# Strassen's algorithm for two of four products in a retention-and-gated-product kernel: one level of it, three stages that share memory, weights by quarters, clamps on ScalarE

## The chip, the cores and the metric

One core of one Trainium2 chip. The metric is the device time of the kernel in microseconds (us). Engines: PE (TensorE, products), DVE (VectorE), ACT (ScalarE), POOL (GpSimd), SP (SyncE, which issues the loads and stores). "Conversion" is what DVE does to the weights: they arrive as 64-bit floats and are turned into 32-bit ones by integer operations, in 40 blocks of 128 x 512.

## The reference

```python
scores = q @ k.T / sqrt(64)              # batch 8, heads 8, sequence 576, head width 64
x = (scores * decay_mask) @ v            # -> 4608 tokens x 512
a, b = x @ w1, x @ w2                    # 512 x 1024 each, float64 in memory
out = ((a * b) @ w3) @ w_out             # 1024 x 1024, 1024 x 512
```

The kernel multiplies w3 by w_out once and uses the product. Attention goes in 4 batch pairs of 5 chunks, 20 turns `g` in all.

## The kernel before: the parts that matter

```python
ld bufs={"k": 2, "q": 1, "v": 3}                # three v buffers

def convert_block():                             # 7 operations on DVE
    e = shift(hi); e = max(e - 896, 0); e = min(e, 255) * 2**23   # two clamps
    e |= sign(hi); m = mantissa(hi); m += lo * 2**-32; w = m * e

def up(i, n, f):                                 # 8 fp32 products of 384 columns
    for w in (w1_sb, w2_sb):
        for c in range(4): matmul(t, w[:, c, f*128:...], xT[:, c, n*384:...])
    scalar.copy(a, ps[0]); vector.tensor_mul(ab[:, f], ps[1], a)

for g in range(20):                              # one turn
    load(g + 2, "kv"); front(g + 1); load(g + 2, "q")
    convert_up_to(...); work(half of the waiting units)
    pv(g); state(g + 1); score(g + 1); work(the other half)
```

`front` multiplies q and v by the decay on POOL and transposes k and q on PE; `pv` is the value product; `work` runs `up` units and `down` groups (the last product) from a list. In the figures below `up` is the w1/w2 product, `po` the last product, `ps` w3 x w_out, `tp` a transpose, `xps` the value product, `sc` the scores, `st` the state.

## Time and profile before

| | before |
|---|---|
| median of 3 runs | 1036.15 us |
| span of the profiled run | 1032.4 us |
| PE busy | 966.2 us |
| end of w3 x w_out (end of the weights' work) | 290.4 us |
| sum of PE's holes before that | 62.5 us |
| sum of PE's holes after it | 0.0 us |

The last three rows come from PE's own instructions: the end of the last `ps`, and the times in which no PE instruction was open (the 3.7 us after PE's last instruction are not counted).

### The profile page before, as it was taken

What the parts mean: (1) busy time and instruction counts of PE and PEld (TensorE: products, weight loads), DVE (VectorE), ACT (ScalarE), POOL (GpSimd) and SP (SyncE); (2) the same over time, 40 slices, a digit from 0 to 9 for tenths busy, and PEclk for the clock granted to TensorE, in tenths of its full rate; (3) what the DMA queues carried; (4) which work ended last, traced back from release to release, by engine and by line L of the source; (5) the groups of instructions that cost most, each with busy time, mean ns of one, the idle gap of its engine ahead of it and who ended that gap; (6) DMA issues with size and microseconds to landing.
All of it is one profiled execution on the core that took longest, in us unless ns stands there. A gap on an engine that the chain in (4) does not pass through costs nothing.

```text
span 1032.4 us, 11355 instructions
## 1 busy us (share of the span) xinstructions
PE 966.2 (94%) x4933; PEld 570.8 (55%) x4933; DVE 269.3 (26%) x475; ACT 144.1 (14%) x285; POOL 78.4 (8%) x47
## 2 busy tenths in 40 slices
PE   4869998498899999999999999999999999999998
PEld 3855565245445565656656555646646545455553
DVE  4898456767800010101110100101101001000010
ACT  2320111011201111111111111202111110010100
POOL 3233010010010100110101101010100000000000
PEclk8888999698999999999999999999999999999999
DMA  7966312252300303212003103113000000000000
GB/s 175 239 171 172 83 50 93 81 143 83 104 29 31 72 1 82 52 31 62 21 11 82 32 11 82 43 40 73 1 21 11 1 31 0 21 11 7 24 0 31
DMA packets 124002, 59.51 MB, mean 58 GB/s; under 512 B 114216, under 2 KB 114216, under 8 KB 123952
## 3 DMA queue, kind: packets, MB, share of 16 engines
q1 hardware_dynamic: 122624, 58.73, 21.2%
q8 instruction: 39, 0.64, 0.3%
q10 hardware_dynamic: 1328, 0.06, 0.1%
q14 instruction: 11, 0.09, 0.0%
HBM read 49.34 MB, written 9.44 MB: 57 GB/s over the span
## 4 chain that ended last, share of the span: by engine, by line
PE 82%; DVE 12%; DMA 3%; issue 1%; SPq 1%; ACT 0%; ACTq 0%; POOL 0%; DVEq 0%; POOLq 0%
PE up L300 44%; PE po L311 24%; PE ps L287 4%; PE xps L196 3%; PE sc L148 3%; DVE e L255 2%; PE tp L133 2%; DMA raw<-in_moe_w_dram 2%; DVE m L260 2%; DVE e L250 2%; PE st L169 1%; DVE m L258 1%; PE xps L189 1%; DVE e L252 1%; DVE e L253 1%; DVE pm L151 1%
## 5 line engine op out<-in xcount | busy, mean ns | idle before, releaser
L300 PE MATMUL up<-xT,w_sb 128*128 128x384 f32 x1536 | 504.6, 489 | 5.4 <-DVE ab L305 5.4
L300 PEld LDWEIGHTS up<-xT,w_sb 128*128 128x128 f32 x1536 | 291.5, 191 | 208.2 <-DVE ab L305 6.6
L311 PE MATMUL po<-w3o,ab 128*128 128x512 f32 x576 | 249.8, 593 | 0.0
L305 DVE TENSOR_TENSOR ab<-up,a 128x384 f32<-128x384 f32 x96 | 53.2, 557 | 576.5 <-PE up L300 576.2
L311 PEld LDWEIGHTS po<-w3o,ab 128*128 128x128 f32 x576 | 109.0, 190 | 134.0 <-issue 130.8
L304 ACT COPY a<-up 128x384 f32<-128x384 f32 x96 | 45.9, 478 | 407.2 <-PE up L300 371.4
L122 POOL TENSOR_TENSOR ld_q<-ld_q,gq 128x1024 f32<-128x1024 f32 (+1 forms) x20 | 38.7, 1935 | 645.3 <-DMA ld_q<-in_q_dram 638.6
L151 DVE TENSOR_TENSOR pm<-sc,mask 128x512 f32<-128x512 f32 (+1 forms) x80 | 45.4, 629 | 134.8 <-PE sc L148 134.8
L287 PE MATMUL ps<-wo,w3T 128*128 128x512 f32 x128 | 60.3, 627 | 1.3 <-ACT w3T L280 1.3
L314 ACT COPY ot<-po 128x512 f32<-128x512 f32 x36 | 21.1, 585 | 250.7 <-PE po L311 230.2
L287 PEld LDWEIGHTS ps<-wo,w3T 128*128 128x128 f32 x128 | 25.3, 203 | 31.2 <-issue 28.3
L133 PE MATMUL tp<-ident,ld_q 128*128 128x128 f32 (+1 forms) x160 | 22.1, 287 | 20.1 <-POOL ld_q L122 20.1
L122 POOL TENSOR_TENSOR ld_v<-ld_v,gk 128x1024 f32<-128x1024 f32 (+1 forms) x20 | 39.5, 1975 | 2.3 <-DMA ld_v<-in_v_dram 2.3
L148 PE MATMUL sc<-qT,kT 64*128 64x128 f32 (+1 forms) x640 | 39.1, 273 | 0.0
L196 PE MATMUL xps<-pm,ld_v 128*64 128x128 f32 (+1 forms) x640 | 37.8, 273 | 0.0
L148 PEld LDWEIGHTS sc<-qT,kT 64*128 64x128 f32 (+1 forms) x640 | 35.4, 183 | 1.5 <-issue 0.5
L196 PEld LDWEIGHTS xps<-pm,ld_v 128*64 128x64 f32 (+1 forms) x640 | 33.4, 143 | 5.0 <-issue 5.0
L278 PE MATMUL tp<-ident,w 128*128 128x128 f32 x64 | 10.7, 303 | 25.2 <-DVE w L262 25.1
L255 DVE SCALAR_TENSOR_TENSOR e<-raw,e 128x512 int32<-128x512 int32 x40 | 32.6, 814 | 1.4
L133 PEld LDWEIGHTS tp<-ident,ld_q 128*128 128x128 f32 (+1 forms) x160 | 18.6, 153 | 21.4 <-POOL ld_q L122 21.4
L200 ACT COPY xT<-xps 128x512 f32<-128x512 f32 (+1 forms) x40 | 19.8, 546 | 73.0 <-PE xps L196 73.0
L260 DVE SCALAR_TENSOR_TENSOR m<-raw,m 128x512 f32<-128x512 uint32 x40 | 27.7, 693 | 1.4
(32 smaller groups left out, 296.8 us busy)
## 6 DMA issues: line engine op xcount, KB each, us to landing
raw<-in_moe_w_dram SPq DMA_DIRECT2D x24, 512.0 KB, 3.6
out_dram<-ot SPq DMA_DIRECT2D x36, 256.0 KB, 2.0
ld_k<-in_k_dram SPq DMA_DIRECT2D x16, 512.0 KB, 4.8
ld_v<-in_v_dram SPq DMA_DIRECT2D x16, 512.0 KB, 5.9
ld_q<-in_q_dram SPq DMA_DIRECT2D x16, 512.0 KB, 4.4
raw<-in_moe_w_dram SPq DMA_DIRECT2D x16, 256.0 KB, 4.9
raw<-in_moe_w_out_dram SPq DMA_DIRECT2D x8, 512.0 KB, 3.2
ld_k<-in_k_dram SPq DMA_DIRECT2D x4, 256.0 KB, 4.9
```

Of the source, the lines that this page charges most:

```text
L122: nc.gpsimd.tensor_tensor(out=t[:sz], in0=t[:sz], in1=gam[:sz, c].rearrange("p b h -> p (b h)").unsqueeze(2).to_broadcast([sz, 2 * H, D]), ...
L133: nc.tensor.transpose(tp[:, p, :sz], src[:sz, h:h + 2, :].rearrange("p a d -> p (a d)"), ident[:sz, :sz])
L148: nc.tensor.matmul(sc[j][:sz, p, :sz], kT[hs, b, p, :sz], qT[hs, b, p, :sz], start=True, stop=True)
L151: nc.vector.tensor_mul(pm[:sz, b, j, :, :sz], sc[j][:sz, :, :sz], mask[:sz, :sz].unsqueeze(1).to_broadcast([sz, NP, sz]))
L196: nc.tensor.matmul(banks[r][heads[half], b, n, :sz], vs[:sz, b * H + 2 * p + j, :], pm[:sz, b, j, p, :sz], start=(c == 0 and m == 0), stop ...
L255: vec.scalar_tensor_tensor(e, in0=hi, scalar=-(1 << 31), in1=e, op0=ALU.bitwise_and, op1=ALU.bitwise_or)
L260: vec.scalar_tensor_tensor(m.bitcast(F32), in0=lo.bitcast(U32), scalar=2.0 ** -32, in1=m, op0=ALU.mult, op1=ALU.add)
L287: nc.tensor.matmul(ps, live["w3T", ft][:, g, :], wo[:, g, :], start=(g == 0), stop=(g == KF - 1))
L300: nc.tensor.matmul(t, w[:, c, f * P:(f + 1) * P], xT[:, c, n * TB:(n + 1) * TB], start=(c == 0), stop=(c == KD - 1))
L304: nc.scalar.copy(a, ps[0])
L305: nc.vector.tensor_mul(live["ab", i, n][:, f, :], ps[1], a)
L311: nc.tensor.matmul(po, ab[:, f, t * P:(t + 1) * P], w3o[:, f, :], start=(f == 0), stop=(f == KF - 1))
```

## The change

Intent: PE bounds most of the run, so give it fewer columns. Strassen's form makes 7 block products out of 8; the sums go to POOL (weights and tokens) and DVE (results). In the code, S names the sums of weight quarters and T those of token quarters; a *unit* is one call of `up`. To find memory for the sums, the kernel runs in three stages whose tiles lie over each other: (1) first pair's attention and all of w1, w2; (2) the rest of the first pair's units, w_out and w3; (3) everything else. Weights are converted by quarters of columns so that units can start early, with two blocks in flight, and two of seven conversion steps go to ACT. The core of the diff, cut:

```diff
-            t = ld.tile(..., bufs={"k": 2, "q": 1, "v": 3}[nm])
+            t = pools["ld"].tile(...)                       # 2 of each
...
+    def strassen_weights(fp):                               # POOL, 512 elements each
+        tt("S1", "A21", "A22", ALU.add);  tt("S2", "S1", "A11", ALU.subtract)
+        tt("S3", "A11", "A21", ALU.subtract);  tt("S4", "A12", "S2", ALU.subtract)
...
-        vec.tensor_scalar(out=e, in0=e, scalar1=-896.0, scalar2=0.0, op0=ALU.add, op1=ALU.max)
-        vec.tensor_scalar(out=e, in0=e, scalar1=255.0, scalar2=2.0 ** 23, op0=ALU.min, op1=ALU.mult)
+        nc.scalar.activation(e, e, relu, bias=lim[:, 0:1], scale=-1.0)
+        nc.scalar.activation(e, e, relu, bias=lim[:, 1:2], scale=-2.0 ** 23)
...
+    def up(i, n, fp, conv=0):                               # a quarter: 28 products of 192
+        p1 = product(None, "A11", "B11");  nc.scalar.copy(p1s, p1)
+        u2 = plus("u2", product(None, "S2", "T2"), p1s)     # plus: DVE, then conv steps
+        u3 = plus("u3", product(None, "S3", "T3"), u2)
+        p5 = product(None, "S1", "T1")
+        plus("c22", p5, u3, out=c[:, 2])
+        plus("c21", product(None, "A22", "-T4"), u3, out=c[:, 1])
+        product(p1, "A12", "B21")                           # first result quarter, DVE
+        product(p5, "S4", "B22");  plus("c12", p5, u2, out=c[:, 0])
+        nc.gpsimd.tensor_tensor(out=ab[:, f + 1:f + 4, :], ...)   # other three, POOL
...
+    for g in range(NC):                                     # stage 1
+            load(g + 2, "kvq")
+        front(g + 1); pv(g); state(g + 1); score(g + 1); convert(10); up(0, 0, g - 1, conv=1); convert(6)
...
     for g in range(NC, G):                                  # stage 3: as before
             load(g + 2, "kv"); front(g + 1); load(g + 2, "q"); work(...); pv(g)
```

A wait that no line of the diff names follows from the first cut: with two v buffers, the load of v for turn g+2 overwrites the v of turn g, so SP holds it until `pv(g)` is done, and SP works in order.

More of the change, by code (lines that the diff above doesn't have):

```diff
@@ L59, with open_attention @@
     NB = 3
-    TB = 2 * S // NB
-    NT = TB // P
+    TB = S // NB
+    NT = 2 * TB // P
     KD = DM // P
     KF = DF // P
+    QC = CV // 2
+    NQ = DF // QC
     heads = [slice(j * D, (j + 1) * D) for j in range(2)]
     const = ctx.enter_context(tc.tile_pool(name="const", bufs=1))
-    raw = ctx.enter_context(tc.tile_pool(name="raw", bufs=2))
-    wst = ctx.enter_context(tc.tile_pool(name="wst", bufs=1))
-    ld = ctx.enter_context(tc.tile_pool(name="ld", bufs=2))
-    fr = ctx.enter_context(tc.tile_pool(name="fr", bufs=2))
-    xp = ctx.enter_context(tc.tile_pool(name="xp", bufs=2))
-    ffn = ctx.enter_context(tc.tile_pool(name="ffn", bufs=2))
+    wp = ctx.enter_context(tc.tile_pool(name="wp", bufs=1))
+    ffn = ctx.enter_context(tc.tile_pool(name="ffn", bufs=2))
+    xps = [ctx.enter_context(tc.tile_pool(name="xp0", bufs=1))]
+    weights_part, att_part, w3_part = ExitStack(), ExitStack(), ExitStack()
+    raw = weights_part.enter_context(tc.tile_pool(name="raw", bufs=2, side="right"))
+    ab3 = weights_part.enter_context(tc.tile_pool(name="ab3", bufs=1, side="right"))
+    pools = {}
+    def open_attention(part):
+        for nm in ("ld", "fr"):
+            pools[nm] = part.enter_context(
+                tc.tile_pool(name=nm, bufs=2, side="right", reuse_waits="tile"))
+    open_attention(att_part)
     acc = ctx.enter_context(tc.tile_pool(name="acc", bufs=7, space=PSUM))
@@ L83 @@
                             base=0, pattern=[[1, P]], channel_multiplier=-1)
+    lim = const.tile([P, 2], F32, tag="lim", name="lim")
+    nc.vector.memset(lim[:, 0:1], 1151.0)
+    nc.vector.memset(lim[:, 1:2], 255.0 * 2.0 ** 23)
     gk = const.tile([P, NC, 2, H], F32, tag="gk", name="gk")
     gq = const.tile([P, NC, 2, H], F32, tag="gq", name="gq")
-    dq = const.tile([H, S], F32, tag="dq", name="dq")
+    dq = ffn.tile([P, 3, 2, TB], F32, tag="c", name="dq").rearrange("p a b s -> p (a b s)")[:H, :S]
     nc.scalar.dma_start(dq, decay_q)
@@ L97, with A, tt @@
             nc.vector.tensor_copy(gq[:sizes[c], c, b, :], gps[:sizes[c], c, :])
-    w1_sb = const.tile([P, KD, DF], F32, tag="w1", name="w1_sb")
-    w2_sb = const.tile([P, KD, DF], F32, tag="w2", name="w2_sb")
-    w3o = const.tile([P, KF, DM], F32, tag="w3o", name="w3o")
-    wo = wst.tile([P, KF, DM], F32, tag="wo", name="wo")
+    halves = range(DF // CV)
+    wA = [wp.tile([P, 2, KD, CV], F32, tag=f"wA{h}", name="wA") for h in halves]
+    wS = [wp.tile([P, 3, 2, 2, 2, P], F32, tag=f"wS{h}", name="wS") for h in halves]
+    def A(fp, nm):
+        h, m = divmod(fp, 2)
+        if nm in ("S1", "S2", "S4"):
+            return wS[h][:, ("S1", "S2", "S4").index(nm), m]
+        r, f = {"A11": (0, 0), "A12": (1, 0), "A21": (0, 1), "S3": (0, 1), "A22": (1, 1)}[nm]
+        return wA[h][:, :, 2 * r:2 * r + 2, m * QC + f * P:m * QC + f * P + P]
+    def strassen_weights(fp):
+        def tt(out, in0, in1, op):
+            nc.gpsimd.tensor_tensor(out=A(fp, out), in0=A(fp, in0), in1=A(fp, in1), op=op)
+        tt("S1", "A21", "A22", ALU.add)
+        tt("S2", "S1", "A11", ALU.subtract)
+        tt("S3", "A11", "A21", ALU.subtract)
+        tt("S4", "A12", "S2", ALU.subtract)
     live = {}
@@ L110, in load @@
         for nm in names:
-            t = ld.tile([P, 2 * H, D], F32, tag="ld_" + nm, name="ld_" + nm,
-                        bufs={"k": 2, "q": 1, "v": 3}[nm])
+            t = pools["ld"].tile([P, 2 * H, D], F32, tag="ld_" + nm, name="ld_" + nm)
             nc.sync.dma_start(
@@ L125, in front @@
                 op=ALU.mult)
-        kT = fr.tile([P, 2, NP, P], F32, tag="kT", name="kT", bufs=1)
-        qT = fr.tile([P, 2, NP, P], F32, tag="qT", name="qT")
+        kT = pools["fr"].tile([P, 2, NP, P], F32, tag="kT", name="kT", bufs=1)
+        qT = pools["fr"].tile([P, 2, NP, P], F32, tag="qT", name="qT")
         for src, dst in ((kn, kT), (qn, qT)):
@@ L142, in score @@
         kT, qT = live["kT", g], live["qT", g]
-        pm = fr.tile([P, 2, 2, NP, P], F32, tag="pm", name="pm", bufs=1)
+        pm = pools["fr"].tile([P, 2, 2, NP, P], F32, tag="pm", name="pm", bufs=1)
         for b in range(2):
@@ L171, in state @@
                                      skip_group_check=True)
-        sb = fr.tile([P, 2, NP, D], F32, tag="sb", name="sb")
+        sb = pools["fr"].tile([P, 2, NP, D], F32, tag="sb", name="sb")
         nc.scalar.copy(sb, st)
@@ L178, in pv @@
         sz = sizes[c]
+        live["x", g] = True
         qT, vs, pm = live["qT", g], live["v", g], live["pm", g]
         if c == 0:
-            live["xT", i] = xp.tile([P, NP, 2, S], F32, tag="xT", name="xT")
+            live["xT", i] = xps[i > 0 and i % 2 == 0].tile([P, NP, 2, S], F32, tag="xT", name="xT")
         banks = [acc.tile([P, 2, 2, P], F32, tag="acc", name="xps") for r in range(2)]
@@ L205 @@
     blocks = []
-    for f0 in range(0, DF, CV):
-        for w_sb, w in ((w1_sb, moe_w1), (w2_sb, moe_w2)):
-            for c in range(KD):
-                blocks.append((("w12", f0, w is moe_w2, c), w, c, f0,
-                               lambda w_sb=w_sb, c=c, f0=f0: w_sb[:, c, f0:f0 + CV]))
-    for g in range(KF):
-        blocks.append((("wo", g), moe_w_out, g, 0, lambda g=g: wo[:, g, :]))
-    for ft in range(KF):
-        for g0 in range(0, DF, CV):
-            blocks.append((("w3", ft, g0), moe_w3, ft, g0,
-                           lambda ft=ft, g0=g0: w3_tile(ft)[:, g0:g0 + CV]))
-    at = {key: n for n, (key, *_) in enumerate(blocks)}
-    loaded, converted, turned = [0], [0], [0]
-    def w3_tile(ft):
-        if ("w3", ft) not in live:
-            live["w3", ft] = wst.tile([P, DF], F32, tag="w3", name="w3")
-        return live["w3", ft]
+    for fp in range(NQ):
+        for j, w in enumerate((moe_w1, moe_w2)):
+            for r in range(2):
+                blocks.append((("w12", fp, j, r), w))
+    blocks += [(("wo", g), moe_w_out) for g in range(KF)]
+    blocks += [(("w3", ft, g0), moe_w3) for ft in range(KF) for g0 in range(0, DF, CV)]
+    at = {key: n for n, (key, _) in enumerate(blocks)}
+    loaded, begun, converted, turned = [0], [0], [0], [0]
     def load_block():
@@ L228, in load_block @@
             return
-        key, w, r, c0, _ = blocks[n]
-        t = raw.tile([P, CV, 2], I32, tag="raw", name="raw")
-        if key[0] == "w12" and r >= NP // 2:
+        key, w = blocks[n]
+        t = raw.tile([P, CV, 2], I32, tag="raw", name="raw", bufs=4)
+        if key[0] == "w12":
+            _, fp, _, r = key
+            src = w[2 * r * P:2 * (r + 1) * P, fp * QC:(fp + 1) * QC, :]
             for half in range(2):
-                o = r * P + (1 - half) * D
-                nc.sync.dma_start(t[heads[half]], w[o:o + D, c0:c0 + CV, :])
+                for_rows = src.rearrange("(c a d) n t -> a d c n t", a=2, d=D)[half ^ r]
+                nc.sync.dma_start(t[heads[half]].rearrange("p (c n) t -> p c n t", c=2), for_rows)
         else:
+            r, c0 = (key[1], 0) if key[0] == "wo" else key[1:]
             nc.sync.dma_start(t, w[r * P:(r + 1) * P, c0:c0 + CV, :])
@@ L238, in load_block, with converted_to, begin_block @@
         loaded[0] += 1
-    def convert_block():
-        n = converted[0]
+    def converted_to(n):
+        key, _ = blocks[n]
+        if key[0] == "w12":
+            _, fp, j, r = key
+            return wA[fp // 2][:, j, 2 * r:2 * r + 2, fp % 2 * QC:fp % 2 * QC + QC]
+        if key[0] == "wo":
+            return live["wo"][:, key[1], :]
+        _, ft, g0 = key
+        if ("w3", ft) not in live:
+            live["w3", ft] = pools["wst"].tile([P, DF], F32, tag="w3", name="w3")
+        return live["w3", ft][:, g0:g0 + CV]
+    def begin_block():
+        n = begun[0]
         t = live["raw", n]
         lo, hi = t[:, :, 0], t[:, :, 1]
-        dst = blocks[n][4]()
-        e = raw.tile([P, CV], I32, tag="exp", name="e", bufs=1)
-        m = raw.tile([P, CV], I32, tag="man", name="m", bufs=1)
+        e = raw.tile([P, CV], I32, tag="exp", name="e")
+        m = raw.tile([P, CV], I32, tag="man", name="m")
         vec = nc.vector
@@ L251, in convert_block @@
                           op0=ALU.logical_shift_left, op1=ALU.logical_shift_right)
-        vec.tensor_scalar(out=e, in0=e, scalar1=-896.0, scalar2=0.0, op0=ALU.add, op1=ALU.max)
-        vec.tensor_scalar(out=e, in0=e, scalar1=255.0, scalar2=2.0 ** 23,
-                          op0=ALU.min, op1=ALU.mult)
+        relu = mybir.ActivationFunctionType.Relu
+        nc.scalar.activation(e, e, relu, bias=lim[:, 0:1], scale=-1.0)
+        nc.scalar.activation(e, e, relu, bias=lim[:, 1:2], scale=-2.0 ** 23)
@@ new lines, in begin_block, with end_block @@
+        yield
+        vec.tensor_scalar(out=m, in0=hi, scalar1=0x000FFFFF, scalar2=0x00100000,
+                          op0=ALU.bitwise_and, op1=ALU.bitwise_or)
+        yield
+        vec.scalar_tensor_tensor(m.bitcast(F32), in0=lo.bitcast(U32), scalar=2.0 ** -32, in1=m,
+                                 op0=ALU.mult, op1=ALU.add)
+        live["em", n] = e, m
+        begun[0] += 1
+        yield
+    def end_block():
+        n = converted[0]
+        hi = live["raw", n][:, :, 1]
+        e, m = live["em", n]
+        vec = nc.vector
@@ L255, in convert_block @@
         vec.scalar_tensor_tensor(e, in0=hi, scalar=-(1 << 31), in1=e,
                                  op0=ALU.bitwise_and, op1=ALU.bitwise_or)
-        vec.tensor_scalar(out=m, in0=hi, scalar1=0x000FFFFF, scalar2=0x00100000,
-                          op0=ALU.bitwise_and, op1=ALU.bitwise_or)
-        vec.scalar_tensor_tensor(m.bitcast(F32), in0=lo.bitcast(U32), scalar=2.0 ** -32, in1=m,
-                                 op0=ALU.mult, op1=ALU.add)
-        vec.scalar_tensor_tensor(dst, in0=m.bitcast(F32), scalar=2.0 ** -20,
-                                 in1=e.bitcast(F32), op0=ALU.mult, op1=ALU.mult)
@@ L264, in convert_block @@
-        converted[0] += 1
-        load_block()
+        yield
+        key = blocks[n][0]
+        while not (key[0] == "w12" or "wo" in live and (key[0] == "wo" or key[1] < turned[0] + 2)):
+            yield "wait"
+        out, m, e = converted_to(n), m.bitcast(F32), e.bitcast(F32)
+        if key[0] == "w12":
+            m, e = (x.rearrange("p (c n) -> p c n", c=2) for x in (m, e))
+        vec.scalar_tensor_tensor(out, in0=m, scalar=2.0 ** -20, in1=e, op0=ALU.mult, op1=ALU.mult)
+        converted[0] += 1
@@ new lines, in end_block, with conversion, convert @@
+        if n > 0:
+            load_block()
+        if key[0] == "w12" and key[2:] == (1, 1):
+            strassen_weights(key[1])
+        yield
+    def conversion():
+        yield from begin_block()
+        while converted[0] < len(blocks):
+            if begun[0] < len(blocks):
+                yield from begin_block()
+            yield from end_block()
+    converting = conversion()
+    def convert(n):
+        for _ in range(n):
+            if next(converting, "wait") == "wait":
+                return
@@ L267, in convert_up_to @@
     def convert_up_to(n):
-        while converted[0] < min(n, len(blocks)):
-            convert_block()
+        while converted[0] < n:
+            assert next(converting, "end") is None
     def w3_tr(ft):
-        convert_up_to(at["w3", ft, DF - CV] + 1)
-        t = wst.tile([P, KF, P], F32, tag="w3T", name="w3T")
+        t = pools["wst"].tile([P, KF, P], F32, tag="w3T", name="w3T")
         for i in range(0, KF, NP):
@@ L279, in w3_tr @@
                                     ident)
-            (nc.scalar.copy if i == 0 else nc.vector.tensor_copy)(t[:, i:i + NP, :], tp)
+            nc.scalar.copy(t[:, i:i + NP, :], tp)
         live["w3T", ft] = t
-        turned[0] = ft + 1
     def w3_mm(ft):
@@ L286, in w3_mm @@
         for g in range(KF):
-            nc.tensor.matmul(ps, live["w3T", ft][:, g, :], wo[:, g, :],
+            nc.tensor.matmul(ps, live["w3T", ft][:, g, :], live["wo"][:, g, :],
                              start=(g == 0), stop=(g == KF - 1))
-        nc.scalar.copy(w3o[:, ft, :], ps)
-    def up(i, n, f):
-        convert_up_to(at["w12", f * P // CV * CV, True, KD - 1] + 1)
-        xT = live["xT", i].rearrange("p n b s -> p n (b s)")
-        if f == 0:
-            live["ab", i, n] = ffn.tile([P, KF, TB], F32, tag="ab", name="ab")
-        ps = []
-        for w in (w1_sb, w2_sb):
-            t = acc.tile([P, TB], F32, tag="acc", name="up")
-            for c in range(KD):
-                nc.tensor.matmul(t, w[:, c, f * P:(f + 1) * P], xT[:, c, n * TB:(n + 1) * TB],
-                                 start=(c == 0), stop=(c == KD - 1))
-            ps.append(t)
-        a = ffn.tile([P, TB], F32, tag="a", name="a")
-        nc.scalar.copy(a, ps[0])
-        nc.vector.tensor_mul(live["ab", i, n][:, f, :], ps[1], a)
+        nc.scalar.copy(live["w3o"][:, ft, :], ps)
@@ new lines, with has_x, strassen_tokens, minus @@
+    every = [(i, n) for i in range(NB2) for n in range(NB)]
+    def has_x(i, n):
+        return any(starts[c] + sizes[c] >= (n + 1) * TB and ("x", i * NC + c) in live for c in range(NC))
+    def strassen_tokens(i, n):
+        x = live["xT", i]
+        B = [[x[:, 2 * r:2 * r + 2, b, n * TB:(n + 1) * TB] for b in range(2)] for r in range(2)]
+        T = [ffn.tile([P, 2, TB], F32, tag="T", name="T", bufs=4) for _ in range(3)]
+        def minus(out, in0, in1):
+            nc.gpsimd.tensor_tensor(out=out, in0=in0, in1=in1, op=ALU.subtract)
+        minus(T[0], B[0][1], B[0][0])
+        minus(T[1], B[1][1], T[0])
+        minus(B[0][1], B[1][1], B[0][1])
+        minus(T[2], B[1][0], T[1])
+        live["B", i, n] = {"B11": B[0][0], "B21": B[1][0], "B22": B[1][1], "T3": B[0][1],
+                           "T1": T[0], "T2": T[1], "-T4": T[2]}
@@ new lines, in up, with product, plus @@
+    def up(i, n, fp, conv=0):
+        m = every.index((i, n))
+        convert_up_to(4 * (fp + 1))
+        if ("B", i, n) not in live:
+            strassen_tokens(i, n)
+        if fp == 0:
+            live["ab", i, n] = (ab3 if m == 2 else ffn).tile([P, 2 * KF, TB], F32, tag="ab", name="ab")
+        ab = live["ab", i, n]
+        f = 4 * fp
+        def product(ps, a, b):
+            a, b = A(fp, a), live["B", i, n][b]
+            new = ps is None
+            if new:
+                ps = acc.tile([P, 2, TB], F32, tag="acc", name="up")
+            for w in range(2):
+                for r in range(2):
+                    nc.tensor.matmul(ps[:, w, :], a[:, w, r, :], b[:, r, :], start=(new and w == r == 0),
+                                     stop=(w == r == 1), skip_group_check=True)
+            return ps
+        def plus(name, ps, sb, out=None):
+            out = ffn.tile([P, 2, TB], F32, tag=name, name=name, bufs=1) if out is None else out
+            nc.vector.tensor_add(out, ps, sb)
+            convert(conv)
+            return out
+        c = ffn.tile([P, 3, 2, TB], F32, tag="c", name="c")
+        p1 = product(None, "A11", "B11")
+        p1s = ffn.tile([P, 2, TB], F32, tag="p1s", name="p1s", bufs=1)
+        nc.scalar.copy(p1s, p1)
+        u2 = plus("u2", product(None, "S2", "T2"), p1s)
[4 more added lines that the diff above has]
+        product(p1, "A12", "B21")
+        c11 = ffn.tile([P, TB], F32, tag="c11", name="c11")
+        nc.scalar.copy(c11, p1[:, 0, :])
+        nc.vector.tensor_mul(ab[:, f, :], p1[:, 1, :], c11)
+        product(p5, "S4", "B22")
+        plus("c12", p5, u2, out=c[:, 0])
+        if fp == NQ - 1 and m + 1 < len(every) and has_x(*every[m + 1]):
+            strassen_tokens(*every[m + 1])
+        nc.gpsimd.tensor_tensor(out=ab[:, f + 1:f + 4, :], in0=c[:, :, 0, :], in1=c[:, :, 1, :], op=ALU.mult)
@@ L307, in down @@
     def down(i, n, t):
-        ab = live["ab", i, n]
+        ab = live["ab", i, n].rearrange("p (f b) s -> p f (b s)", b=2)
         po = acc.tile([P, DM], F32, tag="acc", name="po")
         for f in range(KF):
-            nc.tensor.matmul(po, ab[:, f, t * P:(t + 1) * P], w3o[:, f, :],
+            nc.tensor.matmul(po, ab[:, f, t * P:(t + 1) * P], live["w3o"][:, f, :],
                              start=(f == 0), stop=(f == KF - 1))
-        ot = ffn.tile([P, DM], F32, tag="ot", name="ot")
+        ot = pools["ot"].tile([P, DM], F32, tag="ot", name="ot")
@@ L314, in down @@
         nc.scalar.copy(ot, po)
-        r = i * 2 * S + n * TB + t * P
-        nc.sync.dma_start(out[r:r + P, :], ot)
-    todo = []
-    def add(fn, *args):
-        todo.append(lambda: fn(*args))
-    def add_blocks(i):
-        if i > 0:
-            for n in range(NB):
-                for f in range(KF):
-                    add(up, i, n, f)
-                for t in range(NT):
-                    add(down, i, n, t)
-            return
-        for half in range(2):
-            for n in range(2):
-                for f in range(half * KF // 2, (half + 1) * KF // 2):
-                    add(up, i, n, f)
-        rest = [(up, i, 2, f) for f in range(KF)]
-        add(w3_tr, 0)
-        for ft in range(KF):
-            add(w3_mm, ft)
-            if ft + 1 < KF:
-                add(w3_tr, ft + 1)
-        for n in range(NB):
-            if n == 2:
-                for x in rest:
-                    add(*x)
-            for t in range(NT):
-                add(down, i, n, t)
+        a = t * P
@@ new lines, in down @@
+        while a < (t + 1) * P:
+            b = a // TB
+            e = min((b + 1) * TB, (t + 1) * P)
+            r = (2 * i + b) * S + n * TB + a - b * TB
+            nc.sync.dma_start(out[r:r + e - a, :], ot[a - t * P:e - t * P])
+            a = e
+    load(0, "kqv")
+    load(1, "kqv")
+    for _ in range(4):
+        load_block()
+    front(0)
+    state(0)
+    score(0)
+    for g in range(NC):
+        if g + 2 < NC:
+            load(g + 2, "kvq")
+        if g + 1 < NC:
+            front(g + 1)
+        pv(g)
+        if g + 1 < NC:
+            state(g + 1)
+            score(g + 1)
+        convert(10)
+        if 0 < g < NC - 1:
+            up(0, 0, g - 1, conv=1)
+            convert(6)
@@ new lines @@
+    att_part.close()
+    pools["wst"] = w3_part.enter_context(tc.tile_pool(name="wst", bufs=2, side="right", reuse_waits="tile"))
+    w3op = ctx.enter_context(tc.tile_pool(name="w3op", bufs=1, reuse_waits="tile"))
+    live["wo"] = pools["wst"].tile([P, KF, DM], F32, tag="wo", name="wo", bufs=1)
+    live["w3o"] = w3op.tile([P, KF, DM], F32, tag="w3o", name="w3o")
+    todo = [(0, n, fp) for n in range(NB) for fp in range(NQ)][NC - 2:]
+    multiplied = 0
+    while multiplied < KF:
+        if todo:
+            up(*todo.pop(0), conv=2)
+        if multiplied < turned[0]:
+            w3_mm(multiplied)
+            multiplied += 1
+        if turned[0] < KF and (not todo or converted[0] > at["w3", turned[0], DF - CV]):
+            convert_up_to(at["w3", turned[0], DF - CV] + 1)
+            w3_tr(turned[0])
+            turned[0] += 1
+        convert(10 if not todo else 2)
@@ new lines, with add_pair @@
+    w3_part.close()
+    pools["ot"] = ctx.enter_context(tc.tile_pool(name="ot", bufs=2, reuse_waits="tile"))
+    for t in range(NT):
+        down(0, 2, t)
+    weights_part.close()
+    xps.append(ctx.enter_context(tc.tile_pool(name="xp1", bufs=1, reuse_waits="tile")))
+    open_attention(ctx)
+    todo = [(down, 0, n, t) for n in range(2) for t in range(NT)]
+    def add_pair(i):
+        if i == 1:
+            todo.append((up, 1, 0, 0))
+        for n in range(NB):
+            m = every.index((i, n))
+            todo.extend((up, i, n, fp) for fp in range(1, NQ))
+            if m + 1 < len(every):
+                todo.append((up, *every[m + 1], 0))
+            todo.extend((down, i, n, t) for t in range(NT))
@@ L349, in work @@
     def work(n):
         for _ in range(min(n, len(todo))):
-            todo.pop(0)()
-    load(0, "kqv")
-    load_block()
-    load(1, "kv")
-    load_block()
-    front(0)
-    load(1, "q")
-    state(0)
-    score(0)
-    for g in range(G):
+            fn, *args = todo.pop(0)
+            fn(*args)
+    load(NC, "kqv")
+    load(NC + 1, "kqv")
+    work(1)
+    front(NC)
+    state(NC)
+    score(NC)
+    for g in range(NC, G):
         c = g % NC
@@ L369 @@
             load(g + 2, "q")
-        rows = min(turned[0] + 1, KF)
-        convert_up_to(min(2 * (g + 1) if g < NC else 2 * NC + 6 * (g - NC + 1),
-                          at["w3", rows - 1, DF - CV] + 1))
         work((n + 1) // 2)
@@ L380 @@
         if c == NC - 1:
-            add_blocks(g // NC)
+            add_pair(g // NC)
     work(len(todo))
```

## The prediction

> **What bounds the kernel now.** I read the page's busy shares first, then its 40 slices, then the table of stretches (busy time of each engine, granted clock, DMA share), then the chain of waits in order of time.
>
> ```profile
> PE 966.2 (94%) x4933; PEld 570.8 (55%) x4933; DVE 269.3 (26%) x475; ACT 144.1 (14%) x285; POOL 78.4 (8%) x47
> ...
> PE   4869998498899999999999999999999999999998
> ...
> DVE  4898456767800010101110100101101001000010
> ```
>
> PE is nearly full on average, but the slices split the run in two. For about 11 slices (290 us) PE has holes and DVE is the busy engine: it converts the 64-bit weights, 40 blocks of them. After that DVE is idle and PE has no hole. The table of stretches says it in us:
>
> ```profile
> 25.00:50.00 25.00, 22.18 (x365) 20.33 (x366) 20.41 (x37) 9.42 (x18) 7.58 (x5) 0.84 0.98 230
> 50.00:75.00 25.00, 17.48 (x290) 15.37 (x286) 24.13 (x37) 6.53 (x15) 8.53 (x4) 0.86 0.70 174
> ...
> 175.00:200.00 25.00, 11.55 (x128) 8.34 (x120) 16.20 (x31) 2.72 (x5) 0.00 (x0) 0.80 0.18 63
> ...
> 300.00:782.00 482.00, 482.00 (x2471) 282.44 (x2470) 50.03 (x89) 70.38 (x141) 33.83 (x18) 1.00 0.16 41
> ```
>
> Columns after the length: PE, weight load, DVE, ACT, POOL, granted clock, DMA share, GB/s. From 300 to 782 us PE is busy for all 482.00 us at full clock. There an instruction taken from PE is time taken from the end. The chain gives the true pitch (start to start) of PE's instructions; the durations of the groups (486 to 489 ns for a product's half) overlap and are not it:
>
> ```profile
> 196.28 0.70 DVE m L260
> ...
> 200.18 0.70 DVE m L260
> ...
> 699.33 1.99 PE sc L148 x32
> ...
> 716.99 1.75 PE tp L133 x16
> ...
> 904.94 41.28 PE up L300 x128
> 946.22 20.60 PE po L311 x48
> ```
>
> (Start, length, group.) An fp32 product is two PE instructions. With 384 columns: 41.28/128 = 322.5 ns; with 512: 20.60/48 = 429.2 ns; a 128-column transpose: 1.75/16 = 109.4 ns. All fit columns x 0.833 ns + 2.5 ns. DVE's conversion shows a pitch of 200.18 - 196.28 = 3.90 us a block.
>
> PE's work at these pitches: w1 and w2 products 1536 x 322.5 = 495.4; last product 576 x 429.2 = 247.2; w3 x w_out 128 x 429.2 = 54.9; its transposes 64 x 109.4 = 7.0; attention about 135 (read from the chain, 33.7 for each of four batch pairs). Sum 939.5. The span is 1032.4, so 93 us are lost to holes and cold clock, all before 290 us.
>
> **What the Trainium skill says.** "TensorE: Matmul & The Clock Gate", section "Back-to-back issue gap", has N/2.4 + 2.5 ns for a warm isolated matmul; with two array cycles a column for each half of an fp32 product this is exactly the pitch above, so for 192 columns I get 192 x 0.833 + 2.5 = 162.5 ns. The same page, "LDWEIGHTS", has columns/1.2, 107 ns for 128. The trace records 190 ns for one load, longer than 162.5, so the question is whether a load can become the pitch. It speaks against it: the score products load 128 columns for each 128-column matmul, record 188 ns a load, and two row groups still issue 32 in 1.99 us (a load every 124 ns in each group, tail included). "SBUF — State Buffer", "Who interferes with whom": GpSimd and a VectorE instruction in a two-port mode or with two SBUF inputs lock each other out for the whole instruction. The trace agrees: a 427 ns tensor-scalar took 2005 ns at 21.3 us, when GpSimd's 1998 ns multiply had begun. An add with one input in PSUM is not touched (682 ns beside a GpSimd multiply). "ScalarE: Activation LUTs", "What ACT_TABLE_LOAD costs": 280 ns + 0.833 ns an element with a pointer bias, so an estimated 0.71 us for each clamp; the section on table sets has relu in every set, so no table switches. No run shows that yet.
>
> **The change part by part.**
>
> *Strassen on PE.* Per batch pair and third of tokens, a quarter of the columns was 16 products of 384 columns; it becomes 7 x 4 = 28 products of 192. Columns fall from 6144 to 5376, 7/8. Instructions rise: 12 x 4 x 28 x 2 = 2688 at 162.5 = 436.8 us, against 495.4. Saving 58.6 us; the new PE floor is 939.5 - 58.6 = 880.9. One unit (28 products) is 56 x 162.5 = 9.1 us.
>
> *Evacuation.* Each unit needs on DVE five adds of 384 elements (557 ns, as the present multiply of that shape) and one multiply of 192 (557 - 200 = 0.36): 3.15 us against 1.11. On ACT a copy of 0.48 and one of 0.3; on POOL a multiply of 576 elements. POOL's 1024 elements take 1.94 us, so about 1.1. Per third of tokens POOL adds four subtractions of 384, 0.75 each, and 16 weight combinations of 512, about 1.0 each, once. All of it is under 9.1 us a unit: hidden once conversion is over.
>
> *Clamps to ACT.* A block on DVE goes from 3.90 to about 0.46 + 0.45 + 3 x 0.72 = 3.07 us. 40 blocks save 33 us of DVE, but the 12 units of the first pair give back 12 x (3.15 - 1.11) = 24. DVE in the first two stages: 123 + 38 + mask products 11 = 172 us, plus lock-outs by POOL, about 20.
>
> *Stage 1* (first pair's attention, all of w1 and w2, three units). DVE starts on blocks near 24 us, as it waits for the second chunk. By the end the generator has made 86 of its steps, 16.6 blocks: 86 x 0.61 = 53. Mask products of three chunks 7.5; three units in which DVE waits for PE, about 9 each; waits for POOL's S and T tiles ahead of each unit, 7 + 4 + 3; a wait of 5 for the third chunk; POOL lock-outs 15. The end comes near 24 + 53 + 7.5 + 27 + 14 + 5 + 15, less some 6 of overlap = 140 us.
>
> *Stage 2* (w_out, w3, the other nine units). A turn converts 12 steps = 7.4 us of DVE, + 3.15 + 0.8 lock-out = 11.4. By the counts, the first row of w3 is ready in the fifth turn; five DVE-bound turns = 57. Then four PE-bound turns, 9.1 + 16 x 0.429 (6.9) + 0.9 = 16.9, = 68. Four rows of w3 are left: 30. Stage 2 ends near 295. PE's work by then is 33.7 + 12 x 9.1 + 54.9 + 7 = 205, so some 90 us are lost: about what is lost now. I take 85, as the author's step counts look balanced.
>
> *Stage 3.* Remaining PE work 880.9 - 205 = 676. But while five chunks of the second pair run, only one last-product group (6.9 us) stands beside 7.6 us of attention. The v buffers fall from 3 to 2, so v of the next chunk is requested only after this chunk's value product, and q queues behind it on SyncE. From there: issue 1.3, landing 4 to 5, POOL's multiply 1.95, against 3.8 of PE work: about 3.3 us of hole in each of four or five turns, and 2 + 2 at the seams. About 18 us lost.
>
> Sum: 881 + 85 + 18 = 984 us span; the measured time lies some 2 to 4 above it (1034.25 against 1032.4). As chances of a better stage 1 seem a bit larger than of a worse one, I state 982.
>
> **The rivals.** (a) *The weight load becomes the bound*: if 192 columns do not cover the recorded 190 ns, the products take 2688 x 190 = 511 us, 16 more than now, and the time is about 1055. The score line speaks against it; I give it under 1 in 10. (b) *DVE-bound start grows*: if POOL's locks, late blocks (a block is requested only one block's work ahead) or ACT's order hold DVE to 4.5 us a block, stages 1 and 2 end near 325 and the time is 1012 or so. For it: the DMA was at 98% in the second stretch. Against: stage 2 has no attention loads, and a block there is needed only every 4.8 us. (c) *Start better than now*: if DVE is held less and the clock stays up, stage 2 ends at 260 and the time is 948. (d) *Evacuation stalls in stage 3*: u3 feeds two adds and two PSUM tiles are written twice; the second write to P5 comes 1.8 us after its add ends by my count, so no stall; 1 us in each of 36 units would make 1018.
>
> **Range and chances.** The two firm numbers are PE's -58.6 and its full second part; the start is ±25, the seams ±12. So 982, 948 to 1022 for 8 in 10. Within 2% means above 1015.4: rivals (a), (d) and the worse end of (b), 15 in 100; slower by 2%, only (a) or several together, 4 in 100; faster, 81.
>
> **What would show it.** Right: 128x192 instructions at 162 to 163 ns pitch; PE near 905 us busy; PE idle again until about 290 us with DVE near 90% in the first slices; holes ahead of the q transposes around 320 to 400 us, ended by POOL or the q load; no hole after. Wrong: a pitch of 180 or more; PE waits on DVE adds after 420 us; stage 2 ending before 250 or after 325 us.

## More of the kernel before

The kernel before was run again beside the changed kernel and beside every group of experiments (medians 1037.0, 1034.6, 1034.4 and 1034.4 us), so that a difference of 2 or 3 us between two groups means nothing.

One more piece of the chain of waits (start, length, group), a turn well after conversion, for comparison with the changed kernel:

```profile
336.75 10.32 PE up L300 x32
347.08 1.13 PE tp L133 x16
348.21 26.00 PE up L300 x80
374.20 1.03 PE xps L189 x32
375.24 1.90 PE xps L196 x32
```

The transposes of the next chunk (`tp`) start where the products end, 10.32 + 336.75 = 347.07: their q is long there.

## The result, and the profile after

The changed kernel took 1073.72 us (median of 4, 1072.45 to 1074.96), before 1037.0 beside it: ratio 1.0354, interval 1.0332 to 1.0377. It is 3.5% slower, where 5% faster was forecast. (A ratio is the mean time of one kernel's fast runs over that of the other's of the same rounds, so it is not quite the ratio of the medians.)

The page of the changed kernel, busy shares and slices of PE, DVE and granted clock:

```profile
PE 942.3 (88%) x6085; PEld 743.6 (69%) x6085; DVE 322.8 (30%) x581; ACT 196.2 (18%) x373; POOL 216.5 (20%) x159
...
PE   4456568899999787779898998999989999999998
...
DVE  2445778865500100023112222122122230303120
...
PEclk9767879889999888889999998999999999999999
```

PE has less to do, and more holes: a deeper valley at the start and a new one in slices 14 to 18 (349 to 483 us), where PE had been at 100% before. The table of stretches shows both (columns as in the prediction):

```profile
25.00:50.00 25.00, 12.01 (x148) 10.49 (x148) 9.26 (x18) 8.26 (x13) 3.76 (x2) 0.73 0.71 139
50.00:75.00 25.00, 12.37 (x52) 11.87 (x53) 10.74 (x21) 5.02 (x8) 8.81 (x8) 0.66 0.39 88
...
350.00:375.00 25.00, 18.75 (x203) 13.90 (x200) 3.98 (x8) 6.28 (x13) 6.72 (x4) 0.84 0.77 151
375.00:400.00 25.00, 19.76 (x169) 13.72 (x170) 2.48 (x4) 5.32 (x10) 5.83 (x4) 0.84 0.37 75
400.00:500.00 100.00, 79.99 (x702) 62.34 (x702) 15.87 (x31) 16.01 (x33) 20.32 (x14) 0.87 0.24 50
```

At 25 to 75 us DVE, meant to be the busy engine, works 20 of 50 us; before it worked 44.5. The chain of waits gives the pitch of Strassen's products, and one turn in the valley:

```profile
236.84 9.10 PE up L407 x56
...
375.27 1.97 PE tp L169 x8
377.24 8.75 PE po L442 x16
385.99 1.03 PE xps L226 x32
387.02 1.92 PE xps L233 x32
389.42 6.32 DMA ld_q<-in_q_dram
395.90 1.88 POOL ld_q L158
397.83 1.89 PE tp L169 x8
```

9.10 us / 56 = 162.5 ns: the products run as forecast. The turn goes from transpose to transpose, 397.83 - 375.27 = 22.56 us: the value product ends (388.94), v's load is issued at 389.00 and q's at 389.42, q is on its way for 6.32 us, then POOL multiplies it (1.88), then PE goes on. The piece also shows a lower granted clock: `po` takes 8.75 us, where the first experiments below show 6.87.

The account. PE's floor (its instructions at the full-clock pitch) fell by 58.6. Up to the end of w3 x w_out (319.7 us) the kernel loses 319.7 - 205 = 115 us over its floor, before it lost 93. From there it takes 1073.2 - 319.7 = 753.5 against a floor of 676, so 77.5 more, where before it lost none. -58.6 + 22 + 77.5 = +41, and the spans differ by 40.8. The 77.5 can be divided: PE's holes after 319.7 us sum to 47.4 (five of 5.0 to 6.9 us ahead of q transposes between 369 and 467 us, 30 in all; four of 3.1 to 3.3 after 500 us, 12.7; the rest small); 3.6 us follow PE's last instruction; and the mean granted clock there was 0.964, where it had been 1.00 before, worth about 27 us (an estimate: 0.036 x 750).

### The profile page after: what moved, and what is told of

The parts are those of the page before. It is cut to its first block, busy times and chain, and to the rows that moved or that the text cites. A ratio compares the mean times of both kernels' runs of the same rounds, so it can differ in the third digit from the quotient of the medians.

```text
span 1073.2 us, 14017 instructions
## 1 busy us (share of the span) xinstructions
PE 942.3 (88%) x6085; PEld 743.6 (69%) x6085; DVE 322.8 (30%) x581; ACT 196.2 (18%) x373; POOL 216.5 (20%) x159
## 4 chain that ended last, share of the span: by engine, by line
PE 75%; DVE 8%; DMA 6%; POOL 4%; issue 3%; ACT 2%; SPq 1%; ACTq 0%; POOLq 0%; DVEq 0%
PE up L407 36%; PE po L442 23%; PE ps L365 5%; DMA ld_q<-in_q_dram 4%; PE xps L233 3%; PE tp L169 3%; PE sc L184 2%; POOL ld_q L158 2%; DVE m L302 2%; DVE e L313 1%; PE xps L226 1%; POOL wS L134 1%; SPq L149 1%; PE st L205 1%; DVE m L299 1%
## 5 line engine op out<-in xcount | busy, mean ns | idle before, releaser
L407 PE MATMUL up<-xT,wA 128*128 128x192 f32 x1152 | 225.6, 341 | 18.7 <-DVE wA L322 15.1
L407 PEld LDWEIGHTS up<-xT,wA 128*128 128x128 f32 x1152 | 201.9, 200 | 24.5 <-DVE wA L322 16.3
L436 POOL TENSOR_TENSOR ab<-c 128x576 f32<-128x576 f32 x48 | 69.9, 1455 | 549.6 <-DVE c L413 540.7
L407 PE MATMUL up<-T,wS 128*128 128x192 f32 x768 | 149.0, 339 | 23.6 <-POOL wS L134 14.7
L407 PEld LDWEIGHTS up<-T,wS 128*128 128x128 f32 x768 | 135.1, 200 | 25.3 <-POOL wS L134 15.6
L413 DVE TENSOR_TENSOR c<-up,u 128x384 f32<-128x384 f32 x144 | 80.0, 556 | 77.1 <-PE up L407 76.4
L407 PE MATMUL up<-xT,wS 128*128 128x192 f32 x384 | 72.7, 334 | 5.1 <-DVE c L413 5.1
L407 PE MATMUL up<-T,wA 128*128 128x192 f32 x384 | 70.4, 326 | 1.0 <-ACT ot L445 1.0
L407 PEld LDWEIGHTS up<-xT,wS 128*128 128x128 f32 x384 | 65.1, 194 | 6.5 <-DVE c L413 6.5
L407 PEld LDWEIGHTS up<-T,wA 128*128 128x128 f32 x384 | 63.7, 190 | 1.3 <-ACT ot L445 1.3
```

What stands on the lines that cost most here:

```text
L407: nc.tensor.matmul(ps[:, w, :], a[:, w, r, :], b[:, r, :], start=(new and w == r == 0), stop=(w == r == 1), skip_group_check=True)
L413: nc.vector.tensor_add(out, ps, sb)
L436: nc.gpsimd.tensor_tensor(out=ab[:, f + 1:f + 4, :], in0=c[:, :, 0, :], in1=c[:, :, 1, :], op=ALU.mult)
```

## The experiments

The theory from the trace: (1) *requests*: q stands in SP's queue behind a v that waits for the value product. Rivals: (2) *Strassen's side work* on POOL and DVE; (3) *the cold clock* by itself.

### q and k requested ahead of the value product, in both loops

```diff
-            load(g + 2, "kv"); front(g + 1); load(g + 2, "q"); work(...); pv(g)
+            load(g + 2, "kq"); front(g + 1); work(...); pv(g); load(g + 2, "v")
```

(In the first loop `"kvq"` becomes `"kq"` before and `"v"` after in the same way.)

> The changed kernel with one edit in two loops: q and k of the chunk after next are requested ahead of this chunk's value product, v after it. Theory 1 (the order of requests: with two v buffers, v waits for the value product and q stands behind v): the five holes of 5 to 7 us ahead of the q transposes between 365 and 467 us vanish, a turn there falls from 22.5 us to about 15.5; in the first 60 us the third chunk's scores come about 8 us earlier; together 35 to 60 us less, 1015 to 1040. Rival 2 (POOL is what holds: its sums for Strassen run in order with the q multiply, and lock VectorE out): the holes stay at 5 us or more as POOL is late anyway, and less than 12 us is won, over 1060. Rival 3 (cold clock): the holes go, but the turns stay over 20 us since the clock stays at 0.85.

1033.66 us (ratio to before 0.9981, interval 0.9954 to 1.0008): 40 us less than the changed kernel, equal to the kernel before. The five holes are gone. The part of the expectation on the first 60 us missed: the third chunk's mask products came 2.5 us earlier (43.9 instead of 46.4), not 8.

### The same in the later loop alone

> The same edit in the second loop alone (from the second batch pair on). Theory 1: all of the gain of the late stretch and nothing of the early one: the first 320 us unchanged, 340 to 468 us shrinks by 28 to 40 us; 1033 to 1046. Rival 2: over 1062.

1036.79 us (1.0014, interval 0.9985 to 1.0043). So 37 of the 40 us lie in the later loop. Its turns in the chain, where the holes were:

```profile
370.28 6.87 PE po L442 x16
377.15 1.03 PE xps L226 x32
378.19 1.90 PE xps L233 x32
380.08 0.93 PE st L205 x32
381.02 1.99 PE sc L184 x32
383.00 1.90 PE tp L169 x16
384.90 6.87 PE po L442 x16
...
420.38 1.92 PE xps L233 x32
422.35 5.43 DMA ld_v<-in_v_dram
427.98 1.82 issue
429.79 1.00 POOL T L381
430.86 1.00 POOL T L381
431.91 27.79 PE up L407 x160
```

No DMA and no POOL in the turns: 384.90 - 370.28 = 14.62 us a turn, and `po` is back at 6.87. The clock rises as the holes go (from 365 to 470 us the mean granted clock was 0.84 in the changed kernel, 0.97 in the first experiment), so rival 3 falls as a cause of its own. The last lines show what the edit costs: v now comes late, its multiply stands on POOL ahead of the token sums T, and PE waits 4.4 us for them (5.4 in the first experiment), once. Between the two experiments w3 x w_out ends at 316.8 and 319.2 us, but 2.4 us from the early edit are not clear of noise: a later run (the multiply on VectorE) has the same code up to there and ended at 312.8.

### Strassen alone undone

The `up` of the changed kernel made of 16 plain products of 384 columns; no sums.

```diff
-        p1 = product(None, "A11", "B11") ... plus("c12", p5, u2, out=c[:, 0])
+        for half in range(2):
+            for w in range(2):
+                for k4 in range(4): matmul(t, wA[h][:, w, k4, o:o+128], x[:, k4, :, n*192:...])
+            scalar.copy(a, ps[0]); vector.tensor_mul(ab[:, f+2*half:f+2*half+2], ps[1], a)
```

> The changed kernel with Strassen alone undone: 16 products of 384 columns for a quarter of the columns, evacuated by one copy on ACT and one multiply on VectorE for each half, no sums on POOL; three stages, quarters of columns, clamps on ACT and buffers stay. Theory 1 (Strassen itself pays its 58.6 us of PE, the loss is in the rest of the change): the time rises by 58.6 less what its waits cost (holes ahead of units for POOL's sums some 25 us, the four holes of 3.1 us after 500 us), so 1095, range 1080 to 1130. Rival 2 (Strassen's side work on POOL and VectorE eats its gain): the time stays or falls, under 1075.

1062.52 us (1.0258, interval 1.0232 to 1.0284): 11 us *less* than with Strassen. Theory 1 missed here and rival 2 holds too: the whole 58.6 us that PE gains are eaten by what comes with Strassen. Where: w3 x w_out ends at 285.8 instead of 319.7, although PE has 12 x (10.32 - 9.10) = 14.6 us more to do by then. After it, Strassen is the shorter one by 21 us (753.5 against 1060.5 - 285.8 = 774.7). So it loses beside the conversion and wins later, though less than its ideal 36 x 1.22 = 44.

### The order of requests put into the kernel before

```diff
-            load(g + 2, "kv"); front(g + 1); load(g + 2, "q"); ... pv(g)
+            load(g + 2, "k"); front(g + 1); ... pv(g); load(g + 2, "vq")
```

> The kernel before with the new order of requests put into it and nothing else: v and then q of the chunk after next are requested after this chunk's value product. Theory 1: the late q shows where a turn is short, that is in the first five chunks only (later ones have 40 us a turn): VectorE's start is held, 8 to 25 us more, 1045 to 1061. If the order of requests matters little even there: under 1041.

1045.28 us (1.0093, interval 1.006 to 1.0125), 10.7 us more, and all of it in the start: w3 x w_out ends at 300.8 instead of 290.4, and PE has no hole after it. The same late q costs nothing where a turn takes 39 us or more (from one chunk's q transposes to the next). (Simply giving the kernel before two v buffers can't run: the build stops at a deadlock. In the changed kernel a third v buffer on top of two for k and two for q doesn't fit the memory; with q cut to one buffer, as in the kernel before, it builds, but no run timed it. That other cure stays untested.)

### The three-quarter multiply on VectorE in the later pairs

Four holes of 3.1 to 3.3 us are left after 480 us. The timeline of the first experiment (start, length, engine and line; in brackets the idle time before it):

```profile
481.79 1.04 PE L169 MATMUL tp<-ident,ld_k 128*128 128x128 f32 x8
481.99 0.56 DVE L413 TENSOR_TENSOR c<-up,u 128x384 f32<-128x384 f32 x1 [0.59 <-PE up L407]
...
482.63 1.40 POOL L436 TENSOR_TENSOR ab<-c 128x576 f32<-128x576 f32 x1 [7.69 <-DVE c L413]
483.99 1.90 POOL L158 TENSOR_TENSOR ld_q<-ld_q,gq 128x1024 f32<-128x1024 f32 x1
485.84 1.90 POOL L158 TENSOR_TENSOR ld_v<-ld_v,gk 128x1024 f32<-128x1024 f32 x1
485.94 1.09 PE L169 MATMUL tp<-ident,ld_q 128*128 128x128 f32 x8 [3.11 <-POOL ld_q L158]
```

POOL sat idle for 7.69 us with q at hand (its load had landed at 430.6); in program order the unit's multiply came first, and it waited for PE's last product.

```diff
-        nc.gpsimd.tensor_tensor(out=ab[:, f + 1:f + 4, :], ...)
+        (nc.gpsimd if i == 0 else nc.vector).tensor_tensor(out=ab[:, f + 1:f + 4, :], ...)
```

> The first experiment (q ahead of the value product, both loops) with one more edit: from the second batch pair on, the multiply of three result quarters runs on VectorE instead of GpSimd. Theory: the four holes of 3.1 us ahead of q transposes come from GpSimd's order, where that multiply stands ahead of the q multiply; they vanish, with the cold clock after them 12 to 17 us less: 1016 to 1022. Rival: VectorE's extra multiply (some 0.75 us, two SBUF inputs) delays the adds that PE waits for, or the clock was the cause: under 5 us won, over 1028.

1012.86 us (0.9791, interval 0.9772 to 0.9809): 20.8 us less than without it, more than the range had (1016 to 1022). All four holes are gone. Same place in its trace:

```profile
476.33 1.04 PE L169 MATMUL tp<-ident,ld_k 128*128 128x128 f32 x8
...
477.13 0.76 DVE L436 TENSOR_TENSOR ab<-c 128x576 f32<-128x576 f32 x1
477.21 1.04 PE L169 MATMUL tp<-ident,ld_q 128*128 128x128 f32 x8
```

The profiled run is the fastest of its four; its span is 25.5 us shorter than that of the first experiment. The four holes account for 12.7 of them. Another 4 us lie before the edited part (w3 x w_out ended at 312.8 instead of 316.8, with the same code there) and are noise. The rest is about what the clock gives: after w3 x w_out its mean was 0.981 without the edit and 0.993 with it, worth some 8 us (an estimate: 0.019 x 713 less 0.007 x 692).

### Strassen in the last three pairs only

```diff
+        if i == 0:
+            (plain products as above); return
...
+    for fp in range(NQ): strassen_weights(fp)      # after w3 is done
```

> The first experiment with Strassen kept for the last three batch pairs only: the first pair, which runs beside the conversion of the weights, uses plain products, and the sums of the weights are made after w3 is done. Theory (Strassen's side work costs the first 320 us more than its products save there): the first two stages end near 286 us as in the run without Strassen, the rest takes 717 as in the first experiment: 1000, range 993 to 1010. Rival (what it loses there was the holes alone and returns later, as tokens' and weights' sums now fall in the attention stretch): over 1018.

With q first: 998.88 us (0.9662, interval 0.9644 to 0.9681), as the theory had it (1000), w3 x w_out at 283.1.

### All three edits

> All three edits: q first, plain products in the first pair, the three-quarter multiply on VectorE in the later pairs. If the effects add: 286 + 717 - 15 = 988, range 978 to 998; that beats the kernel before by 4 to 5%. If they share one cause: over 1000.

977.16 us (0.9455, interval 0.9436 to 0.9474), 5.5% faster than the kernel before and correct. The time lies just below the range (978 to 998), since the multiply was worth 20.8 and not 15. The two effects on top of the first experiment are -20.8 and -34.8, together -55.6; measured -56.5: they add. Its page:

```profile
PE 923.4 (95%) x5797; PEld 681.4 (70%) x5797; DVE 323.7 (33%) x569; ACT 197.6 (20%) x373; POOL 135.5 (14%) x99
...
PE   5577889999998999899999999999999999999998
```

### Strassen without its sums (a wrong result)

The products read plain quarters of weights and tokens in place of S and T; adds, multiplies and requests as in the changed kernel.

```diff
-            return wS[h][:, ("S1", "S2", "S4").index(nm), m]      # and strassen_weights, minus(...) left out
+        r, f = {"S1": (0, 1), "S2": (1, 1), "S4": (1, 0), ...}[nm]
```

> The changed kernel with the sums of weights and of tokens left out (a wrong result on purpose): the seven products read plain quarters in their place; same products, same adds on VectorE, same multiply on GpSimd, same requests. If GpSimd's sums are what Strassen costs the start (waits for S and T of 5 to 9 us ahead of the first four units, VectorE locked out): the first two stages end at 285 to 300 instead of 320 us, 1035 to 1055 in all. If it is VectorE's adds (3.15 us a unit against 1.1): they end over 310 us, over 1060 in all.

1048.63 us (1.0152, interval 1.0123 to 1.0182). w3 x w_out ends at 291.3, so the sums cost the start 28.4 us by the two traces; after it nothing changes (752.7 against 753.5). The four runs spread over 6.8 us and the profiled one is the fastest; by the medians it is 25.1 us. This is what the changed kernel's group showed as idle PE time:

```profile
L407 PE MATMUL up<-T,wS 128*128 128x192 f32 x768 | 149.0, 339 | 23.6 <-POOL wS L134 14.7 <-POOL T L381 8.9
```

Of 34 us between Strassen and plain products in the start the sums are 25 to 28. Plain products have 14.6 more of PE and still end 5.5 earlier, so some 20 us are left for the adds, POOL's multiply and the changed order together; these were not separated.

### Plain products with q first

> Strassen undone (plain products everywhere) together with the first experiment's order of requests. If the two add: 1062.5 less the 40 us that the order was worth with Strassen, 1022, range 1015 to 1032; and against the best version (977) some 45 us more, which is what 36 units of Strassen are worth where their side work is hidden (36 x (10.32 - 9.10) = 44). If the order is worth less without Strassen: over 1035.

1014.69 us (0.9811, interval 0.9795 to 0.9827), 48 less than without the edit, just under the range. So everything of the change but Strassen, with the requests in order, is worth about 2%; which part of it (stages, quarters, clamps) was not separated. Against it the best version's Strassen in 36 units gains 37.5 us of its ideal 44.

### The clamps on ScalarE in the kernel before

```diff
-        (the two clamps as tensor_scalar on VectorE)
+        nc.scalar.activation(e, e, relu, ...) twice; the combine moved behind the mantissa
```

> The kernel before with the two clamps of each weight block on ScalarE and nothing else (the combine moved behind the mantissa so that ScalarE has time). If VectorE's time bounds the start: 40 x 0.4 to 0.9 us less on VectorE, of which some 5 to 20 us come through: 1015 to 1030. If the start is bound by requests and the first products: within 4 us of 1034.

1094.02 us (1.0593, interval 1.0553 to 1.0633): a plain miss, 60 us slower. Its list of waits says why:

```profile
DVE e L262 <- ACT e L257: 85.7, 37, 11.0
...
PE tp L280 <- DVE w L264: 62.0, 16, 11.0
```

DVE waited for ACT in 37 of 40 blocks, 85.7 us, up to 11.0 at once. At 212.7 us of its trace the cause can be read: the clamp stands on ACT behind the copy of `ps`, which waits for PE, until 218.6; DVE waits 7.9 us for the clamp, and PE then 3.6 us for DVE's block. In the changed kernel the combining step never waited for ACT; it has the next block's first half in flight, which my edit had not. So the run doesn't price the change's clamps. That the two-block pipeline is what saves them there is argued; no run tested it.

## Why the prediction was wrong, point by point

- *PE's saving.* Right: 162.5 ns pitch forecast, 162.5 measured; the weight load did not become the bound (rival a falls).
- *Stage 3, "about 3.3 us of hole in each of four or five turns ... About 18 us lost".* The mechanism was found ahead of the run and is confirmed by the experiments in both kernels (in the one before, in its first part alone); its size was not, and this is the largest term that failed: 77.5 us were lost in place of 18. Holes of 5.0 to 6.9 us stood in five turns. In the chain q took 6 to 8 us from issue to landing, not "4 to 5" (v's load is under way at the same time; whether that is why was not tested). I took PE's 14.5 us at full clock, and it was granted 0.84 to 0.87 there. A turn was 22.5 us, not 17.8, and moving the request gave 37 us.
- *"All of it is under 9.1 us a unit: hidden once conversion is over."* This step failed too. It compared POOL's load with PE's and left out POOL's order: the unit's multiply ends after the unit and stands ahead of the q multiply that PE needs next. Taking it off POOL gave 20.8 us.
- *Stages 1 and 2, "Stage 2 ends near 295".* 319.7 in the trace. DVE's work was forecast well (172 + 20 us; 190.7 in the trace up to there); its waits were not. The terms "7 + 4 + 3" ahead of the first three units were 8.9 + 4.9 + 4.9, a fourth wait of 4.9 stood ahead of the fourth unit, and in all the sums cost 25 to 28 us. I had sized POOL's sums by its multiply of 1024 elements (1.9 ns each); the weight sums took 1.26 us instead of 1.0, the token ones 1.0 instead of 0.75, the unit's multiply 1.4 instead of 1.1.
- *The wait of "5 for the third chunk".* The mask products of the third chunk began at 46.4 us after 15.6 idle us on DVE. The early edit took only 2.5 us off that, so what the wait costs stays open.
- *Rival (b)*, a longer start, came true in size (320 against 325), though by the sums, which an experiment shows, and not, as far as tested, by late blocks; *(d)*, stalls of the adds within the units of stage 3, did not come: the holes there stand where units meet attention, and with the multiply on DVE the four are gone. I gave 15 in 100 for a time within 2% and 4 in 100 for a slower one, as if one thing would go wrong at a time; the longer start and two kinds of holes came together and added up.
- *The signs named ahead.* The pitch and the holes ahead of the q transposes came. DVE near 90% in the first slices (20 to 80%), PE busy near 905 us (942.3) and "no hole after" did not.

## What to carry to other kernels

Fewer products on the bound engine paid here only where the extra sums lay beside spare time of the other engines: 12 Strassen units put the end of w3 x w_out back by 34 us beside the conversion, and the other 36 won 37.5 us once their multiply was off POOL. When a change cuts a buffer, list what now stands in the same queue behind the load that waits for it; moving one request ahead gave 37 us and took no memory. When holes are forecast on PE, look at the granted clock too: here some 27 us went with it. Before calling an engine's work hidden, ask not only how long it is but what the bound engine needs next from the same queue.

## What the Trainium skill lacked or had wrong

- "TensorE: Matmul & The Clock Gate", sections "Back-to-back issue gap" and "LDWEIGHTS": the formula, which the page gives for an isolated matmul, held in streams with two array cycles a column for each of the two instructions of an fp32 product, at 128, 192, 384 and 512 columns (109.4, 162.5, 322.5, 429.2 ns); those sections do not give the fp32 case (another page counts four passes, without a pitch). A recorded load of 190 ns is not its pitch: 192-column products with a new load each still came every 162.5 ns.
- "GPSIMD Engine Reference", section "Elementwise — side-by-side cycle accounting": its 2.6 cycles an element (2.17 ns at 1.2 GHz) are near what POOL's two-input operations show, 1.00 us for 384 and 1.40 us for 576 elements (2.1 ns for each more), where my estimate from this trace's multiply by a broadcast operand (1024 in 1.9 us) was too low. That a broadcast operand makes it cheaper an element is not on that section, and no run here tested it.
- "SBUF — State Buffer", section "Who interferes with whom": agrees (a 0.69 us VectorE operation with two SBUF inputs took 2.27 beside POOL). What cost more here is POOL's order, 20.8 us, which is not a matter of the ports.
- "ScalarE: Activation LUTs", section "What ACT_TABLE_LOAD costs": the estimate of 0.71 us for a clamp was right (0.72), and no table switch was seen beyond the one load near the start that both kernels have.
